# One operation for a softmax step's scaling, a planner that lands loads later, and a second unit's token loads held back, in a planned single-core attention and mixture kernel

## The chip, the cores and the metric

The kernel runs on 1 core of one Trainium2 chip. The metric is the device time of one launch in microseconds (us); lower is better. Before the change three runs gave 815.47, 816.01 and 816.30 us, a median of 816.01 us.

## What is computed

```python
def reference(**kwargs):
    attn_out = _attn_ref(**attn_kwargs)              # 4 x 8 heads x 576 tokens x 64, causal, window 64
    x = attn_out.transpose(0, 2, 1, 3).reshape(2304, 512)
    h = x @ w_in                                     # 2304 x 512 @ 512 x 2048
    P = a[0] + a[1]*h + a[2]*h**2 + a[3]*h**3
    Q = 1.0 + abs(b[0])*abs(h) + abs(b[1])*h**2
    x = (P / (Q + 1e-06)) @ w_out                    # 2048 x 512
    return ((x @ w1) * (x @ w2) @ w3) @ wo2          # 512 x 1024 twice, 1024 x 1024, 1024 x 512
```

## The kernel before, in words

All large products run in split form: each operand is a high part and a low part (a rounded copy and the remainder), and a product is three matmuls (high by high, high by low, low by high).

**Attention and first layer.** Ten units of tokens with four pairs of heads each make 40 attention steps, taken two at a time. A step is: load k, q and v; S, the scores (`sp`, L612); per window of 128x128 a masked copy on DVE with its row minimum (L615) and an exponential on ACT with its row sum (L621); once for two steps a sum on POOL (L554) and a reciprocal on DVE (L557); then the scaling `nm` of each window by that reciprocal, on ACT (L626) or, for the first 16 steps only, on POOL (L628); T, the transpose (`tp`, L633); its copy on ACT (L638); O, the product with v (`op`, L564); and at the end of the two steps the high part x on ACT (L574) and the low part on DVE (L577). A step has 3 windows (tokens in blocks of 384) or 4 (blocks of 512).

The first layer goes over five blocks of tokens (384, 384, 512, 512, 512) and 16 chunks of the hidden dimension for each, two chunks making a pair: 40 pairs. H (`hp`, L689) computes hidden values into PSUM; ACT and DVE evaluate P/Q (L701, L706, L711, L714, L717, L726, L730 to L756). `hi` (L745 or L747) writes the high part of the value to `g[:,0]`, `d` (L754 or L756) computes the remainder's factor `u`, and `lo` (L761) writes the low part `g[:,1] = u * r`. Blocks of 384 have two `lo` of 128x384 for a pair, each on DVE or POOL; in four of the blocks of 512 a flag `whole` makes it one DVE operation of 128x1024. D (`acc`, L767) sums g @ w_out in PSUM, and evictions (L841, L847 and ACT) bring the result to DRAM as `x2d`. In the meantime the weights are split by ACT and DVE (`wt`, L447 to L463), partly stored back to DRAM as `kw` and `kb`.

**Second layer.** w3 @ wo2 is formed first (W: `wp`, L934). Then 768 tokens at a time make a unit u = 0, 1, 2. P(u) forms x @ w1 and x @ w2 in a form with seven products in place of eight (`pa`, `pb`, `pc`, L1079): for each n = 0..7 two stored halves of the weights are loaded ("first" and "second", `wc<-kw`, L1036), and the blocks `bs<-kb` (L1040), from which DVE makes sums `ss` (L1047). The tokens come as four blocks B12, B11, B22 and B21 (`xf`, L1006), split on ACT (L1010) and DVE (L1013), and their sums T1 to T4 (L975) replace them in their buffers. The product of the two results goes through R (L1206) to the output. The order is P0, P1, R0, R1, P2, R2. Sums of the W product are stored and reloaded (`wsum`, L1146).

**What sets the order.** Nothing is reordered at run time. A planner (class `Plan`) holds every operation with its candidate engines, a cost, a `tail` (how long after its end a load's reader may start), an optional due time and the ring of buffers that it fills. It draws noise on the due times from a seeded generator, runs its own list schedule forwards and backwards for some rounds, and keeps the shortest. The result is one fixed order of instructions for each engine. SP issues all DMAs, in that order: a DMA whose buffer or source isn't ready holds every DMA behind it.

```python
rng = Random(60)
due = [d + rng.gauss(0.0, 0.5) for d in dues(preds)]
```

Of the kernel before, what the change touches and what calls it, by code (L numbers as in the profile page):

```python
# [65 lines left out]
class Plan:  # L66
# [30 lines left out]
    def order(self, rounds=16):  # L97
# [125 lines left out]
        rng = Random(60)  # L223
# [21 lines left out]
def body(ctx: ExitStack, tc: tile.TileContext, qkv, kv0, qk0, w_in, w_out, a, b, w1, w2, w3t, wo2, out):  # L245
# [51 lines left out]
    op("c", (("D", 0.95),), constants, tail=2.2, due=8.0)  # L297
# [25 lines left out]
    BEFORE = {NF * PAIRS[t + 1][0] + PAIRS[t + 1][1]: [("O", i + 1) for i in now if i % NP] for t, now in AT.items() if now and t >= 16 and t + 1 < NI}  # L323
# [58 lines left out]

    UN = NT // (2 * T_)
# [44 lines left out]
    def conv(name, dst, n, src, tag, due=None, spare=False, pre=None, kept=None):  # L428
# [62 lines left out]
        op((name, n, "load"), (("D", 1.72),), load, after=["swap"] if spare else [], new=(ws,), tail=2.2, due=due)  # L491
# [40 lines left out]
    def attn(pair):  # L532
# [46 lines left out]
        def step(k):  # L579
# [62 lines left out]
            op(("load", i), (("D", (0.48 if k else 1.12) if thin else 1.1 * wide),), load, after=[("load", i0)] if thin and k else (), new=(kb_,) if thin and k else (kb_, qb), uses=(qb,) if thin and k else (), tail=2.2)  # L642
            op(("loadv", i), (("D", 0.66 * wide),), loadv, after=(("load", i),), new=(vb,), tail=2.2)
# [27 lines left out]
    def chunks(c0):  # L671
# [9 lines left out]
        whole = j >= G  # L681
# [135 lines left out]
    def evacuate(j, part, then):  # L817
# [99 lines left out]
    SPARE = [("w3", 0), ("w3", 2)]  # L917
# [78 lines left out]
    def tokens(u):  # L996
# [24 lines left out]
        for i, (b, (k, h)) in enumerate(where.items()):  # L1021
            j = 2 * u + h
            op(("xl2", u, b), (("D", 1.3),), lambda _, b=b: load(b), after=["swap2"] + [("store", i, int(i in HALVED), n) for n in (2 * k, 2 * k + 1) for i in range(NB) if START[i] < (j + 1) * T_ and START[i] + TOKENS[i] > j * T_], new=(fb[b],), tail=2.2, turn=seq["P", u, 0, 1] - 20.0 + i)
        seven((u,), f, fb, {b: ("xl2", u, b) for b in where}, split)

    def weights(u, n):
# [31 lines left out]
        for i in range(2):  # L1058
            op(("sw", u, n, i), (("D", 1.72),), lambda _, i=i: load(i), after=[(("w1", "w2")[i], n, "keepw"), "swap2"], new=(wbs[i],), tail=2.2)
# [284 lines left out]
```

## Time and profile before

| | us |
|---|---|
| three runs | 815.47, 816.01, 816.30 |
| the profiled execution's own time | 815.19 |
| its span in the trace | 813.4 |
| TensorE (PE) busy | 785.7 (97%) |
| VectorE (DVE) busy | 728.7 (90%) |
| ScalarE (ACT) busy | 553.1 (68%) |
| GpSimd (POOL) busy | 50.1 (6%) |
| mean granted TensorE clock | 0.992 |

The span runs from the first to the last instruction. Busy time is the time in which an engine has an instruction in hand; PE's part is modelled and holds matmuls that overlap. The granted clock is a share of 2.4 GHz: 0.5 is 1.2 GHz, and a window's mean says how much of it was at either level. Idle time is named by what ended it. SP has no busy time of its own; what counts there is when it issues.

### The profile page before, as it was taken

The numbers are of one execution on the slowest core, as the hardware profiler recorded it, in microseconds if no ns is written. First come the engines' busy times: TensorE is split into PE (matmuls) and PEld (weight loads), VectorE is DVE, ScalarE is ACT, GpSimd is POOL, SyncE is SP. The second block draws the span as 40 slices with busy tenths as digits, with TensorE's granted clock in tenths as the row PEclk, the third lists the DMA queues.
The fourth block names the chain that finished last, engine by engine and source line by source line (L and its number), as shares of the span: only waits on it lengthen the run. The fifth ranks groups of instructions, "written<-read, shape, count | busy, mean of one in ns | idle before, by whom it ended". The sixth has DMA issues, their size and how long they took to land.

```text
span 813.4 us, 13444 instructions
## 1 busy us (share of the span) xinstructions
PE 785.7 (97%) x4728; PEld 718.9 (88%) x4728; DVE 728.7 (90%) x1340; ACT 553.1 (68%) x1182; POOL 50.1 (6%) x74
## 2 busy tenths in 40 slices
PE   5879999999999999999999999998999999999998
PEld 4669999888899999888788888888999999999998
DVE  7899999999997999999999998997999798847754
ACT  6888998768999999766477781376565447444434
POOL 2231120001210100000000000000000000000000
PEclk9899999999999999999999999999999999999999
DMA  8977984333167675545763356868979685136402
GB/s 295 337 259 251 306 295 162 119 124 104 64 208 229 222 219 192 180 166 196 288 218 132 143 199 214 306 207 274 316 276 318 234 282 175 64 121 212 156 1 77
DMA packets 64099, 165.51 MB, mean 203 GB/s; under 512 B 7200, under 2 KB 24608, under 8 KB 64032
## 3 DMA queue, kind: packets, MB, share of 16 engines
q1 hardware_dynamic: 64032, 164.66, 59.2%
q8 instruction: 37, 0.61, 0.3%
q14 instruction: 30, 0.25, 0.1%
HBM read 123.21 MB, written 41.42 MB: 202 GB/s over the span
## 4 chain that ended last, share of the span: by engine, by line
PE 86%; DVE 9%; DMA 2%; ACT 2%; issue 1%; POOL 0%; SPq 0%; POOLq 0%; DVEq 0%
PE acc L767 22%; PE hp L689 21%; PE pb L1079 9%; PE pa L1079 6%; PE pc L1079 6%; PE wp L934 5%; PE pb L1206 5%; PE pc L1206 3%; PE pa L1206 3%; PE sp L612 2%; PE tp L633 1%; PE op L564 1%; DMA wc<-kw 1%; DVE wt L453 1%; DMA ws<-in_w_in 1%; DVE u L756 1%
## 5 line engine op out<-in xcount | busy, mean ns | idle before, releaser
L689 PE MATMUL hp<-x,wc 128*128 128x512 f32 (+1 forms) x960 | 220.1, 374 | 3.0 <-DVE u L717 3.0
L767 PE MATMUL acc<-g,wc 128*128 128x512 f32 (+1 forms) x960 | 215.0, 371 | 4.4 <-POOL g L761 3.6
L767 PEld LDWEIGHTS acc<-g,wc 128*128 128x128 f32 x960 | 174.3, 188 | 28.9 <-POOL g L761 4.0
L689 PEld LDWEIGHTS hp<-x,wc 128*128 128x128 f32 x960 | 174.9, 190 | 26.6 <-DVE u L717 3.9
L1079 PE MATMUL pb<-xb,wc 128*128 128x384 f32 x432 | 86.0, 336 | 0.3 <-ACT u L1087 0.3
L1079 PEld LDWEIGHTS pb<-xb,wc 128*128 128x128 f32 x432 | 76.5, 189 | 0.7 <-ACT u L1087 0.6
L621 ACT ACTIVATE sm<-sm,st 128x128 f32<-128x128 f32 x144 | 56.4, 400 | 18.3 <-DVE st L615 18.2
L730 ACT ACTIVATE r<-qa,cq 128x1024 f32<-128x1024 f32 (+1 forms) x40 | 42.9, 1072 | 30.7 <-DVE qa L726 16.9
L711 ACT ACTIVATE u<-hp,ca 128x512 f32<-128x512 f32 (+1 forms) x80 | 59.5, 745 | 3.0 <-PE hp L689 3.0
L1079 PE MATMUL pa<-xb,wc 128*128 128x384 f32 x288 | 58.1, 339 | 2.5 <-DMA wc<-kw 2.5
L706 ACT ACTIVATE qa<-hp,cb 128x512 f32<-128x512 f32 (+1 forms) x80 | 51.7, 646 | 12.7 <-PE hp L689 12.1
L1079 PE MATMUL pc<-xb,wc 128*128 128x384 f32 x288 | 57.3, 334 | 0.0
L1168 ACT ACTIVATE rt<-prod 128x768 fp32r<-128x768 f32 x42 | 35.6, 847 | 31.5 <-PE pa L1206 10.3
L1171 DVE TENSOR_TENSOR rt<-prod,rt 128x768 fp32r<-128x768 f32 x42 | 40.1, 956 | 16.6 <-ACT rt L1168 16.1
L701 ACT ACTIVATE h<-hp 128x512 f32<-128x512 f32 (+1 forms) x80 | 44.5, 556 | 14.0 <-PE hp L689 11.1
L1079 PEld LDWEIGHTS pa<-xb,wc 128*128 128x128 f32 x288 | 51.3, 191 | 3.0 <-ACT ww L943 2.8
L460 ACT ACTIVATE wc<-wt 128x512 fp32r<-128x512 f32 x48 | 30.1, 633 | 32.9 <-DVE wt L453 23.5
L726 DVE SCALAR_TENSOR_TENSOR qa<-h,cab,qa 128x1024 f32<-128x1024 f32 (+1 forms) x40 | 47.4, 1185 | 4.6 <-ACT qa L706 3.7
L1079 PEld LDWEIGHTS pc<-xb,wc 128*128 128x128 f32 x288 | 50.5, 188 | 0.0
L450 DVE SCALAR_TENSOR_TENSOR wt<-ws,wt 128x512 uint32<-128x512 uint32 x72 | 50.0, 697 | 0.4
L453 DVE SCALAR_TENSOR_TENSOR wt<-ws,wt 128x512 uint32<-128x512 uint32 x72 | 49.2, 686 | 0.3
L612 PE MATMUL sp<-k,q 64*64 64x128 f32 (+1 forms) x384 | 40.7, 297 | 8.5 <-DMA k<-in_kv 6.3
(86 smaller groups left out, 1370.6 us busy)
## 6 DMA issues: line engine op xcount, KB each, us to landing
wc<-kw SPq DMA_DIRECT2D x48, 512.0 KB, 5.3
bs<-kb SPq DMA_DIRECT2D x24, 512.0 KB, 4.4
ws<-in_w_in SPq DMA_DIRECT2D x16, 512.0 KB, 5.4
ws<-in_w_out SPq DMA_DIRECT2D x16, 512.0 KB, 4.8
ws<-in_w SPq DMA_DIRECT2D x16, 512.0 KB, 4.5
kw<-ws SPq DMA_DIRECT2D x16, 512.0 KB, 3.2
ws<-in_w3t SPq DMA_DIRECT2D x16, 512.0 KB, 4.5
wsum<-wsum SPq DMA_DIRECT2D x16, 512.0 KB, 5.7
```

The source lines that it names most:

```text
L450: stt(out=x["b"], in0=x["st"][:, :, 0], scalar=29, in1=x["b"], op0=ALU.logical_shift_right, op1=ALU.bitwise_or)
L453: stt(out=x["b"], in0=x["st"][:, :, 1], scalar=0xC0000000, in1=x["b"], op0=ALU.bitwise_and, op1=ALU.bitwise_or)
L612: nc.tensor.matmul(sp[h, w, :], x["q"][h, w], x["k"][h, kat[w] * W_:kat[w] * W_ + P], start=True, stop=True)
L621: act(x["sm"][:, m, :], x["sm"][:, m, :], AF.Exp, bias=col(0, k, m), scale=-1.0, accum_out=col(1, k, m))
L689: nc.tensor.matmul(x["hp", m], wf_(win, f0 + m)[:, s_, kk * P:(kk + 1) * P], (xh, xl)[m_][xk][:, kk, :], start=(kk == 0 and i == 0), stop= ...
L701: act(x["h2"][:, m, :], x["hp", m], AF.Square)
L706: act(x["qa"][:, m, :], x["hp", m], AF.Abs, scale=b0)
L711: act(x["u"][:, m, :], x["hp", m], AF.Identity, scale=a3, bias=a2)
L726: stt(out=x["qa"], in0=x["h2"], scalar=b1, in1=x["qa"], op0=MUL, op1=ADD)
L767: nc.tensor.matmul(accs[j, part, n], wf_(wout, f0 + m)[:, s_, n * P:(n + 1) * P], x["g"][:, m_, m, :], start=(first and i == 0), stop=(las ...
L1079: nc.tensor.matmul(x[m], sws[u, n, i0][:, s_, (c0 + k) * P:(c0 + k + 1) * P], t[:, m_, k, :], start=(first and k == 0 and i == 0), stop=(k ...
L1206: nc.tensor.matmul(x[m, n], w[:, s_, (c + n) * P:(c + n + 1) * P], rts[u, b, r][:, m_, k, :], start=(first and r == 0 and k == 0 and i == ...
```

## The change

The scaling of a step becomes one operation in the plan, on one engine: ACT (still one instruction for each window), or one `tensor_tensor` over all windows on POOL or DVE, with the reciprocals broadcast. `whole` becomes False, so the low part of a pair of 512 tokens is two operations, each on DVE or POOL. The planner gets `tail=3.0` for loads in place of 2.2, another seed, other places of the attention steps among the pairs (`AT`), no O steps placed ahead of the following H (`BEFORE`), earlier due times for evictions, other due times for the `wsum` sums and w2, and another spare buffer. The loads of the second unit's tokens (u = 1) may not be issued before the second half-load of n = 3 of the first unit (`XL = 3`). What is computed stays the same; every engine's order changes. Nearly all of the code moves down by one line, L628 and after by two for a few lines (the scaling on POOL is L630).

```diff
-        rng = Random(60)
+        rng = Random(65)
...
-        AT[((-8, -6, -4, -2), (0, 1, 2, 3), (4, 5, 6, 7), (15, 16, 17, 18), (20, 22, 24, 26))[j][r // 2]].append(i)
+        AT[((-8, -6, -4, -2), (0, 1, 2, 3), (4, 5, 6, 6), (16, 18, 19, 20), (22, 24, 25, 26))[j][r // 2]].append(i)
...
-    BEFORE = {... for t, now in AT.items() if now and t >= 16 and t + 1 < NI}
+    BEFORE = {... for t, now in AT.items() if now and t >= 99 and t + 1 < NI}
...
-            def nm(m, e):
-                r, t = col(3, k, m), x["sm"][:, m, :]
+            def nm(e):
+                r = y["st"][:, 2 * NW * 3 + NW * k:2 * NW * 3 + NW * k + NW]
                 if e == "A":
-                    act(t, t, cp, scale=r)
+                    for m in range(NW):
+                        act(x["sm"][:, m, :], x["sm"][:, m, :], cp, scale=r[:, m:m + 1])
                 else:
-                    nc.gpsimd.tensor_scalar(out=t, in0=t, scalar1=r, scalar2=1.0, op0=MUL, op1=MUL)
+                    engine[e].tensor_tensor(out=x["sm"], in0=x["sm"], in1=r.unsqueeze(2).to_broadcast([P, NW, P]), op=MUL)
...
-            for m in range(NW):
-                op(("nm", i, m), (("A", 0.32), ("P", 0.52)) if i < 16 else (("A", 0.32),), lambda e, m=m: nm(m, e), after=(("rc", i0),), uses=(sb, mb))
+            op(("nm", i), (("A", 0.32 * NW), ("P", 0.97 * wide), ("V", cost(0.065, 0.40))), nm, port=True, after=(("rc", i0),), uses=(sb, mb))
...
-        whole = j >= G
+        whole = False
...
-            due = seq[then[:-1] + (n,)] - 0.7
+            due = seq[then[:-1] + (n,)] - 1.4
...
-    SPARE = [("w3", 0), ("w3", 2)]
+    SPARE = [("w3", 0), ("w3", 5)]
...
-            op(("xl2", u, b), (("D", 1.3),), ..., after=["swap2"] + [("store", ...) ...], new=(fb[b],), tail=2.2, turn=...)
+            op(("xl2", u, b), (("D", 1.3),), ..., after=["swap2"] + ([("sw", 0, XL, 1)] if u == 1 else []) + [("store", ...) ...], new=(fb[b],), tail=3.0, turn=...)
...
-            op(("sw", u, n, i), (("D", 1.72),), lambda _, i=i: load(i), after=[...], new=(wbs[i],), tail=2.2)
+            op(("sw", u, n, i), (("D", 1.72),), lambda _, i=i: load(i), after=[...], new=(wbs[i],), tail=3.0)
...
-        due = seq["P", 0, 1, 1] + 8.0 * i
+        due = seq["P", 0, 1, 1] + 6.0 * i
...
-        conv("w2", w2c, n, w2[n], None, pre=231.0 + 32.0 * n, kept=1)
+        conv("w2", w2c, n, w2[n], None, pre=231.0 + 35.0 * n, kept=1)
```

All other loads get `tail=3.0` in the same way.

In the whole program the change turns 123 scaling windows on ACT into 80, and 21 on POOL into none; 12 whole-step scalings appear on DVE (5 of 128x384, 7 of 128x512) and 6 on POOL (3 and 3). Of the low parts, DVE has 35 of 128x512 in place of 16 of 128x1024 and 11 of 128x512, and 10 of 128x384 in place of 16; POOL has 22 of 128x384 in place of 16 and 13 of 128x512 in place of 5. PE's matmuls are the same in number and shape.

Three places show how the order moves. On SP, at the start of P(0), where the loads of the second layer's weights are issued (`kw2` is the stored weights of n = 2, `bs` its blocks, `xf` tokens), before:

```order
L1036 DMA wc_5605<-kw0_2804 128x1024
...
L1006 DMA xf_5681<-x2d_58 128x2x384
...
L1040 DMA bs_5703<-kb1_2869 128x1024
L1036 DMA wc_5722<-kw1_2892 128x1024
L1036 DMA wc_5741<-kw0_2804 128x1024
L1040 DMA bs_5808<-kb2_3226 128x1024
L1036 DMA wc_5831<-kw2_3311 128x1024
L1036 DMA wc_5847<-kw1_2892 128x1024
L1006 DMA xf_5872<-x2d_58 128x2x384
L1146 DMA wsum00_5888<-wsum_5822 128x1024
L1036 DMA wc_5912<-kw3_3747 128x1024
```

and now:

```order
L1041 DMA bs_5642<-kb1_2750 128x1024
L1037 DMA wc_5658<-kw1_2774 128x1024
L1037 DMA wc_5671<-kw0_2668 128x1024
L1007 DMA xf_5686<-x2d_58 128x2x384
L1037 DMA wc_5754<-kw2_3102 128x1024
L1041 DMA bs_5770<-kb2_3002 128x1024
L1037 DMA wc_5792<-kw1_2774 128x1024
L1147 DMA wsum00_5817<-wsum_5780 128x1024
L1147 DMA wsum01_5836<-wsum_5783 128x1024
L1037 DMA wc_5859<-kw3_3660 128x1024
```

The first load of `kw2` stood behind the blocks `bs` of n = 2 and stands ahead of them now; `xf_5872` of the second unit is gone from here (its first row comes 13 rows behind the last one shown), and the last block of the first unit, `xf_5686`, has moved behind the second load of `kw0`.

On PE, the rows ahead of the first two `acc` of the program, before:

```order
L612 MATMUL sp<-k,q 64x128 x12
L689 MATMUL hp<-x,wc 128x384 x15
L633 MATMUL tp<-idn,sm 128x128 x3
L689 MATMUL hp<-x,wc 128x384 x3
L633 MATMUL tp<-idn,sm 128x128 x3
L689 MATMUL hp<-x,wc 128x384 x6
L564 MATMUL op<-sm,v 64x64 x24
L689 MATMUL hp<-x,wc 128x384 x6
L612 MATMUL sp<-k,q 64x128 x12
L767 MATMUL acc_805<-g,wc 128x384 x3
L767 MATMUL acc_812<-g,wc 128x384 x3
```

and now:

```order
L613 MATMUL sp<-k,q 64x128 x12
L690 MATMUL hp<-x,wc 128x384 x18
L635 MATMUL tp<-idn,sm 128x128 x6
L565 MATMUL op<-sm,v 64x64 x24
L690 MATMUL hp<-x,wc 128x384 x15
L613 MATMUL sp<-k,q 64x128 x12
L690 MATMUL hp<-x,wc 128x384 x21
L768 MATMUL acc_839<-g,wc 128x384 x3
L768 MATMUL acc_849<-g,wc 128x384 x3
```

From the program's start to its first `acc` PE had 48 `hp` matmuls and has 72 now, with the same 84 scores, 36 transposes and 72 products with v.

On DVE, the rows from a pair's `d` on whose low part POOL computes (`g_2173` before, both halves of the pair of `u_3806` now), before:

```order
L750 SCALAR_TENSOR_TENSOR qa_2093<-qa_2093,g_2173 128x1024
L447 TENSOR_SCALAR wt_2196<-ws_1731 128x512
L756 SCALAR_TENSOR_TENSOR u_2048<-u_2048,ca_63,qa_2093 128x1024
L447 TENSOR_SCALAR wt_2209<-ws_2055 128x512
L761 TENSOR_TENSOR g_2173<-u_2048,r_2151 128x512
L714 TENSOR_TENSOR u_2204<-u_2204,hp_2132 128x512
```

and now:

```order
L757 SCALAR_TENSOR_TENSOR u_3806<-u_3806,ca_63,qa_3819 128x1024
L616 ISA sm_3959,st_3942<-sp_3958,mask_77 128x128
L616 ISA st_3942 128x1
...
L718 SCALAR_TENSOR_TENSOR u_3932<-u_3932,ca_63,hp_3880 128x512
L715 TENSOR_TENSOR u_3932<-u_3932,hp_3919 128x512
```

DVE had a conversion and its own half of the low part behind `d`, both on SBUF operands; it has masked copies out of PSUM there now (four of them, two of which are left out with their second rows), and both halves are on POOL.

## Rows read from the trace of the kernel before

**Rows 1.** The page, part 1: busy time, share and instructions of each engine.
```profile
PE 785.7 (97%) x4728; PEld 718.9 (88%) x4728; DVE 728.7 (90%) x1340; ACT 553.1 (68%) x1182; POOL 50.1 (6%) x74
```
**Rows 2.** Windows: each engine's busy time, PE's granted clock, DMA share and GB/s.
```profile
0.00:60.00 60.00, 41.00 (x410) 34.31 (x411) 51.26 (x166) 47.90 (x156) 17.00 (x40) 0.91 0.84 295
60.00:90.00 30.00, 30.00 (x245) 28.97 (x244) 27.53 (x75) 26.17 (x77) 4.60 (x8) 1.00 0.81 280
90.00:110.00 20.00, 18.43 (x162) 16.97 (x161) 19.90 (x51) 18.58 (x57) 3.47 (x4) 1.00 0.84 287
110.00:340.00 230.00, 230.00 (x1464) 209.03 (x1464) 221.99 (x432) 198.97 (x470) 24.99 (x23) 1.00 0.52 172
340.00:350.00 10.00, 9.22 (x97) 7.29 (x96) 10.00 (x14) 6.48 (x11) 0.00 (x0) 1.00 0.59 204
350.00:550.00 200.00, 199.94 (x891) 166.18 (x890) 195.30 (x256) 122.74 (x185) 0.00 (x0) 1.00 0.58 206
550.00:560.00 10.00, 7.48 (x35) 7.19 (x34) 7.06 (x16) 6.32 (x14) 0.00 (x0) 0.83 0.99 311
600.00:610.00 10.00, 9.73 (x56) 9.41 (x56) 9.92 (x19) 6.96 (x14) 0.00 (x0) 1.00 0.81 279
```
**Rows 3.** Timeline of PE, 540 to 562 us; idle time ahead in brackets.
```profile
550.11 2.25 PE L1079 MATMUL pb<-xb,wc 128*128 128x384 f32 x12
554.88 2.26 PE L1079 MATMUL pa<-xb,wc 128*128 128x384 f32 x6 [2.52 <-DMA wc<-kw]
```
**Rows 4.** Timeline of SP's queue, 500 to 560 us: start and length of issues.
```profile
534.31 0.85 SPq L1036 DMA_DIRECT2D wc<-kw  x2
545.20 0.32 SPq L1040 DMA_DIRECT2D bs<-kb  x1
545.61 1.68 SPq L1036 DMA_DIRECT2D wc<-kw  x2
547.40 0.37 SPq L1006 DMA_DIRECT2D xf<-x2d  x1
```
**Rows 5.** Waits of SP's queue, 533 to 556 us: total, times, longest.
```profile
SPq L1040 <- DVE ss L1047: 6.0, 1, 6.0
SPq L1040 <- DMA bs<-kb: 3.9, 1, 3.9
```
**Rows 6.** The chain that ended last, 535 to 562 us: start, length, what.
```profile
545.61 9.13 DMA wc<-kw
```
**Rows 7.** Groups by line and form: busy us, mean ns of one.
```profile
L626 ACT ACTIVATE sm<-sm,st 128x128 f32<-128x128 f32 x123 | 39.3, 401 | 0.2
L628 POOL TENSOR_SCALAR sm<-sm,st 128x128 f32<-128x128 f32 x21 | 10.3, 504 | 4.9 <-DVE st L557 4.9
L761 DVE TENSOR_TENSOR g<-u,r 128x1024 fp32r<-128x1024 f32 x16 | 19.5, 1220 | 0.0
L761 DVE TENSOR_TENSOR g<-u,r 128x384 fp32r<-128x384 f32 x16 | 9.5, 613 | 0.0
L761 DVE TENSOR_TENSOR g<-u,r 128x512 fp32r<-128x512 f32 x11 | 7.8, 732 | 0.0
L761 POOL TENSOR_TENSOR g<-u,r 128x384 fp32r<-128x384 f32 x16 | 17.3, 1088 | 84.6 <-DVE u L756 50.5 <-DVE u L754 32.8 <-DVE st L557 1.1
L761 POOL TENSOR_TENSOR g<-u,r 128x512 fp32r<-128x512 f32 x5 | 7.5, 1516 | 69.5 <-DVE u L756 28.4 <-ACT u L711 20.7 <-DVE u L754 20.4
L447 DVE TENSOR_SCALAR wt<-ws 128x512 uint32<-128x512 uint32 x72 | 31.6, 442 | 0.8 <-DMA ws<-in_w_in 0.6 <-DMA ws<-in_w 0.2
```
**Rows 8.** Timeline, 195 to 200 us: start, length, engine, line.
```profile
195.88 3.06 POOL L761 TENSOR_TENSOR g<-u,r 128x512 fp32r<-128x512 f32 x2 [20.44 <-DVE u L754]
...
197.71 1.52 DVE L447 TENSOR_SCALAR wt<-ws 128x512 uint32<-128x512 uint32 x1
```
**Rows 9.** Timeline of PE at two gaps before 110 us.
```profile
55.94 1.90 PE L767 MATMUL acc<-g,wc 128*128 128x384 f32 x6 [2.94 <-POOL g L761]
...
92.57 2.35 PE L689 MATMUL hp<-x,wc 128*128 128x384 f32 x12 [0.42 <-DVE u L717]
```

More of the change, by code (lines that the diff above doesn't have):

```diff
@@ L321, in body @@
     TS, TT, TO, TOO = 0.67, 0.33, (0.71, 0.42), 1.9
-    BEFORE = {NF * PAIRS[t + 1][0] + PAIRS[t + 1][1]: [("O", i + 1) for i in now if i % NP] for t, now in AT.items() if now and t >= 16 and t + 1 < NI}
+    BEFORE = {NF * PAIRS[t + 1][0] + PAIRS[t + 1][1]: [("O", i + 1) for i in now if i % NP] for t, now in AT.items() if now and t >= 99 and t + 1 < NI}
     seq = {}
@@ L489, in keepw @@
             nc.sync.dma_start(out=kw[n][:, kept], in_=x["w"].bitcast(F32))
-        op((name, n, "load"), (("D", 1.72),), load, after=["swap"] if spare else [], new=(ws,), tail=2.2, due=due)
+        op((name, n, "load"), (("D", 1.72),), load, after=["swap"] if spare else [], new=(ws,), tail=3.0, due=due)
         op((name, n, "b0"), (("V", 0.34),), b0_, port=True, after=((name, n, "load"),), new=(wt,), uses=(ws,), turn=None if due is None else due + 4.0)
@@ L499, in conv @@
                 op((name, n, "keepd"), (("D", 1.72),), keepd, after=((name, n, "lo"),), uses=(wc,), tail=2.0, due=seq["H", NF + n, 0])
-                op((name, n, "second"), (("D", 1.72),), second, after=((name, n, "keepd"),), new=((tag, (name + "2", n)),), tail=2.2)
+                op((name, n, "second"), (("D", 1.72),), second, after=((name, n, "keepd"),), new=((tag, (name + "2", n)),), tail=3.0)
         else:
@@ L861, in evacuate @@
                 after.append(("evl", j, n))
-                op(("evl", j, n), (("D", 0.66 * ev_cost),), lambda _, n=n: load(n), after=(("store", j, 0, n), "swap"), new=(vb,), tail=2.2)
+                op(("evl", j, n), (("D", 0.66 * ev_cost),), lambda _, n=n: load(n), after=(("store", j, 0, n), "swap"), new=(vb,), tail=3.0)
             elif more:
@@ L865, in evacuate @@
                 if n % 2 == 0:
-                    op(("evl", j, n // 2), (("D", 1.3 * ev_cost),), lambda _, n=n: load(n), after=(("store", j, 0, n), ("store", j, 0, n + 1)), new=(vb,), tail=2.2)
+                    op(("evl", j, n // 2), (("D", 1.3 * ev_cost),), lambda _, n=n: load(n), after=(("store", j, 0, n), ("store", j, 0, n + 1)), new=(vb,), tail=3.0)
             new = new and not more
@@ L1022, in tokens @@
             j = 2 * u + h
-            op(("xl2", u, b), (("D", 1.3),), lambda _, b=b: load(b), after=["swap2"] + [("store", i, int(i in HALVED), n) for n in (2 * k, 2 * k + 1) for i in range(NB) if START[i] < (j + 1) * T_ and START[i] + TOKENS[i] > j * T_], new=(fb[b],), tail=2.2, turn=seq["P", u, 0, 1] - 20.0 + i)
+            op(("xl2", u, b), (("D", 1.3),), lambda _, b=b: load(b), after=["swap2"] + ([("sw", 0, XL, 1)] if u == 1 else []) + [("store", i, int(i in HALVED), n) for n in (2 * k, 2 * k + 1) for i in range(NB) if START[i] < (j + 1) * T_ and START[i] + TOKENS[i] > j * T_], new=(fb[b],), tail=3.0, turn=seq["P", u, 0, 1] - 20.0 + i)
         seven((u,), f, fb, {b: ("xl2", u, b) for b in where}, split)
@@ L1160, in wc_sums @@
             op(("wsk", i, q), (("D", 1.72),), lambda _, q=q: keep(q), after=(("wsp", i, q),), uses=(wbs[q],), tail=2.0, due=due + 6.0)
-            op(("wsl", i, q), (("D", 1.72),), lambda _, q=q: again(q), after=(("wsk", i, q),), new=(("wa", ("wsum", i, q)),), tail=2.2, turn=seq["R", 0, 1, 0, 0] + 4 * q + i)
+            op(("wsl", i, q), (("D", 1.72),), lambda _, q=q: again(q), after=(("wsk", i, q),), new=(("wa", ("wsum", i, q)),), tail=3.0, turn=seq["R", 0, 1, 0, 0] + 4 * q + i)
     rts = {}
```

15 lines of the change are left out of this document (8 added, 7 removed).

## The prediction

> **What bounds the kernel now.** I read the busy shares first, then the windows, then PE's timeline at the places where the windows show PE idle, and last the queue that the idle time points to. PE is busy for 785.7 of 813.4 us [rows 1], and the windows say where the rest lies [rows 2]: 19.0 us of idle time in the first 60 us, 1.57 in 90 to 110, 0.78 in 340 to 350, 2.52 in 550 to 560, 0.27 in 600 to 610; from 110 to 340 there is none, from 350 to 550 only 0.06. The reader should see two things. Work taken off any other engine gains nothing where PE is full, so this change can gain only at those five places. And PE's clock costs besides: a mean of 0.91 over the first 60 us and of 0.83 from 550 to 560 [rows 2], 2.4 GHz in part and 1.2 GHz in part; in the second window (1 - 0.83) x 10 = 1.7 us of full-speed work is lost. DVE is second: 222.0 of 230 us in 110 to 340 and 195.3 of 200 in 350 to 550 [rows 2]. It makes the values that PE's `acc` needs and has little room to be late.
>
> The profiled execution took 815.19 us, 0.8 under the median of 816.01. I add the terms to 815.19 and then these 0.8.
>
> **The place that decides: 552 to 560 us.** PE ends a row of `pb` at 552.36, waits 2.52 us for `wc<-kw`, and resumes at half clock: six matmuls take 2.26 us there [rows 3], where twelve take 2.25 ahead of the wait. The load is the first one of n = 2. It was issued only at 545.61 and took 9.13 us to land [rows 4, 6]. The issue was late because SP had been silent since 535.2 [rows 4]: it stood before the `bs` load of n = 2, for 3.9 us because of a DMA and for 6.0 us because of DVE's sums `ss` [rows 5]. The load of `kw2` behind it needs neither. The change puts that load ahead of the `bs` in SP's order, and takes the second unit's `xf`, which went out at 547.40 into the same traffic [rows 4], out of this stretch. With nothing blocked ahead of it, it can be issued about when SP came free before, at 535 to 536. If it lands as slowly as it did, in 9.13 us, it is there at 545, and its matmuls are due at about 551 to 552. So the wait goes, and the clock with it: 2.52 + 1.7 = **4.2 us**. The bounds: nothing, if another load is late in its place; 4.2 at most, as there is no more idle time in this window. What is late next: the second load of n = 1 is still queued behind the blocked `bs`, and the first unit's last block B21, whose load now comes after the second load of `kw0`, is needed after some 6 us more of DVE's work than before. I give back 0.5 us for these (0 to 4.2).
>
> **The scaling and the low parts.** ACT loses 43 windows of 0.401 us, 17.2 us [rows 7]. ACT is not what PE waits for after 110 us, so this is worth nothing there. DVE: 16 whole low parts go (19.5 us), 24 halves come (24 x 0.732 = 17.6), 6 of 128x384 go (6 x 0.613 = 3.7), and 12 scalings come, which no row shows; a multiplication of that size out of SBUF is the low part itself, so 5 x 0.613 + 7 x 0.732 = 8.2 [rows 7]. That makes DVE 2.6 us longer; the scalings read one operand broadcast, so I bound each between half and twice that price (-1.5 to +10.8). POOL gains 9 x 1.088 + 11 x 1.516 = 26.5 us and loses 10.3 [rows 7]; its share stays small, but a low part on POOL ends 0.4 to 0.8 us later than on DVE, in the path from `d` to `acc`. I priced every instruction of both orders by its own row's duration and compared DVE's work up to a pair's `d` with PE's work up to that pair's first `acc`. The largest lag is the same (17.6 us before, in the first pair, 17.7 now, in the seventh); it grows by 1 to 5 us in the pairs 5 to 22 (11.6 to 16.4 in pair 7) and shrinks by 4 to 6 in the pairs 23 to 26. The latter removes the 0.78 us at 340 to 350 (**-0.8**; 0 to 0.8). The former runs through the stretch in which PE has no idle time but the 1.57 us of 90 to 110, two waits of which are 0.42 for DVE [rows 9] and 0.64 for POOL: I take **+0.7** (-1.6, if that idle time goes, to +4).
>
> By the rows POOL also holds DVE up. While two low parts of 128x512 ran on POOL from 195.88 to 198.94, a conversion on DVE took 1.52 us [rows 8], in place of the 0.442 of its kind [rows 7]. At the places where POOL takes a low part, a DVE operation on SBUF operands alone stands among the first two behind `d` in 6 of 16 cases before and in 6 of 22 now; in the others there are operations that read PSUM. At 1.1 us each that is the same on both sides, so I add nothing; the other end, POOL's longer work of 26.5 - 10.3 = 16.2 us passed on to DVE in full, is a rival below. The Trainium skill (SBUF — State Buffer, SBUF: two separate sides) says that DVE and GpSimd share a pair of ports under an exclusive lock, so that a DVE operation with two SBUF inputs, or in a 2-port mode, stands still for the whole of a GpSimd operation. The trace agrees at 197.71; by this rule, wherever such an operation is next, all that POOL gains is DVE's loss.
>
> **The start.** In the first 60 us DVE and ACT run almost without a pause (51.3 and 47.9 us busy [rows 2]), and PE waits for them. Priced the same way, DVE's work up to the third pair of tokens' `x` grows from 23.2 to 25.2 us, which starts the first `hp` that needs it 2.0 us later, and up to the first `d` from 45.4 to 47.9. Against this PE has 24 more `hp` ahead of the first `acc`. Twelve take 2.2 us [rows 9], so these are 4.4 us of work, in a place where PE waited 2.94 us and then ran at half clock (six `acc` in 1.90 us [rows 9]). The first `acc` was at 55.94; with these 4.4 us of work done it would have been at 60.3, or at 62.0 with the same 1.7 us of clock as at 552. For the change I find the first `acc` at 60.9: the sixth chunk's `hp`, behind DVE's fourth operation on `u`, starts at about 58.7 by the same pricing, and 2.2 us of work follow. With part of the low clock remaining I take **-0.5** (-3 to +2.5). The earlier evictions, the spacing of `wsum` and of w2, and the other spare buffer move operations on engines and queues with room while PE is full: nothing, as long as no buffer comes free late.
>
> **P(0) to P(1).** The second unit's tokens are issued some 15 to 30 positions later on SP. Three of the four blocks stay about ten us ahead of their need; the last is as tight as it was, and PE waited 0.27 us there [rows 2]: 0 (0 to 4).
>
> **Sum:** -4.2 + 0.5 - 0.8 + 0.7 - 0.5 = -4.3 us on 815.19, so 810.9, and **811.7** as a median.
>
> **Rivals.**
> - **DVE comes too late from 60 to 340 us (chance 0.16; slower).** The scalings on DVE, the longer low parts on POOL and the lags that are up by 1 to 5 us open waits ahead of `acc`. For: DVE is busy 96% of this stretch, and waits of that kind exist at 90 to 110. Against: the largest lag is unchanged, and PSUM reads stand beside POOL now. It decides where a `d` comes over some 2 us later against PE than before. If five or six pairs wait 1.2 us each, that is +7 us in place of +0.7, so 818.0.
> - **POOL holds DVE up in full (0.04; slower).** As at 197.71 [rows 8], but for the whole 16.2 us, of which about half shows on PE, since the other half falls to `d`s that are early: 811.7 + 8 = 819.7. For: DVE's full windows leave no empty place. Against: the order puts PSUM reads beside POOL. It is what the Trainium skill's rule (SBUF — State Buffer, SBUF: two separate sides) would give without that order.
> - **The wait at 552 us is only moved (0.13; same).** The second load of n = 1 or the split of B21 comes as late as `kw2` did. For: both still hang on the same DVE sums. Against: more PE work lies ahead of them. Nothing is gained there: 811.7 + 3.7 = 815.4.
> - **The held tokens are late at the second unit (0.07; same).** A load of 9.13 us [rows 6] that misses its place by 2.5 us costs what it did at 552, a wait and the clock, 4.2 us: 815.9.
> - **The start gains more (part of the forecast).** If the 2.94 us wait and its clock go, 809.
>
> **Numbers.** Forecast 0.60, all of it faster. About 0.2% (1.6 us) is what a measurement of this kernel can tell from no change. The rivals give 0.20 slower and 0.20 about the same, of which I move 0.02 to faster and 0.01 to slower, because part of a gap may stay. The range reaches from 808.0 (start and 90 to 110 us gain in full) to 818.0 (the first rival); the forecast's own range is 808.5 to 814.
>
> **What would show it.** Right: no idle time and clock 1.00 in the windows between 540 and 570 us; SP issues the first `kw2` load before the blocked `bs`; PE's idle time to 60 us at 18 to 20; none at 340 to 350; ACT's scaling near 26 us in place of 39.3. Wrong: new waits of PE for `g` or `u` between 60 and 340 us that sum to over 3 us; a wait for `xb` or `wc` and a clock under 1.00 somewhere between 540 and 620; or more idle time or a lower clock in the first 60 us than 19.0 and 0.91.

## The result, and the profile after

The changed kernel took 807.72 us (median of 4 runs, 806.66 to 808.58) against 816.15 before (4 runs): a ratio of 0.9894, 95% interval 0.9877 to 0.9911, a gain of 8.4 us. The forecast was 811.7 us, its range 808.0 to 818.0: the direction was right, the forecast gain of 4.3 us about half of what came, and the time lies just below the range. On two of the chips of the experiments the changed kernel gave 808.35 against 814.95 (e5: 0.9911, interval 0.9893 to 0.9928) and 807.20 against 815.04 (e15: 0.9904, 0.9884 to 0.9923), 6.6 and 7.8 us.

The windows of the changed kernel, with the columns of [rows 2]; the profiled execution took 807.59 us, its span was 805.8:

```profile
0.00:60.00 60.00, 40.72 (x412) 32.90 (x413) 52.05 (x167) 46.71 (x151) 7.85 (x23) 0.94 0.84 290
60.00:90.00 30.00, 30.00 (x244) 29.15 (x243) 29.74 (x74) 26.44 (x73) 6.58 (x9) 1.00 0.85 296
90.00:110.00 20.00, 20.00 (x179) 19.65 (x178) 20.00 (x61) 19.33 (x59) 2.11 (x4) 1.00 0.89 305
110.00:340.00 230.00, 229.12 (x1450) 207.28 (x1449) 223.01 (x432) 189.38 (x430) 33.29 (x33) 1.00 0.50 169
340.00:350.00 10.00, 10.00 (x104) 8.39 (x103) 9.12 (x13) 9.92 (x22) 0.00 (x0) 1.00 0.35 125
350.00:540.00 190.00, 189.88 (x839) 156.69 (x838) 186.76 (x256) 114.55 (x170) 7.66 (x6) 1.00 0.63 221
540.00:570.00 30.00, 30.00 (x173) 29.78 (x172) 29.35 (x60) 20.95 (x42) 0.00 (x0) 1.00 0.85 291
600.00:620.00 20.00, 20.00 (x117) 20.00 (x116) 18.88 (x38) 10.38 (x20) 0.00 (x0) 1.00 0.87 302
```

PE has no wait and its full clock from 540 to 570; the waits of 90 to 110, 340 to 350 and 600 to 610 are gone too. New are 0.88 us between 110 and 340 and 0.12 from 350 to 540. The first 60 us hold 19.3 us of idle time in place of 19.0. SP issues the first load of `kw2` at 530.08, ahead of the `bs` (SP's queue of the changed kernel):

```profile
530.08 0.42 SPq L1037 DMA_DIRECT2D wc<-kw  x1
538.75 0.32 SPq L1041 DMA_DIRECT2D bs<-kb  x1
```

The groups that the change touches (line, engine, operation, shape; busy us, mean ns), against [rows 7]:

```profile
L628 ACT ACTIVATE sm<-sm,st 128x128 f32<-128x128 f32 x80 | 25.5, 397 | 0.6 <-DVE st L558 0.5
L630 DVE TENSOR_TENSOR sm<-sm,st 128x512 f32<-128x512 f32 x7 | 4.8, 684 | 0.0
L630 DVE TENSOR_TENSOR sm<-sm,st 128x384 f32<-128x384 f32 x5 | 2.8, 551 | 0.0
L630 POOL TENSOR_TENSOR sm<-sm,st 128x512 f32<-128x512 f32 x3 | 3.7, 1220 | 0.8 <-DVE st L558 0.8
L630 POOL TENSOR_TENSOR sm<-sm,st 128x384 f32<-128x384 f32 x3 | 2.5, 832 | 2.1 <-DVE st L558 2.1
L762 DVE TENSOR_TENSOR g<-u,r 128x512 fp32r<-128x512 f32 x35 | 24.0, 719 | 0.1
L762 POOL TENSOR_TENSOR g<-u,r 128x384 fp32r<-128x384 f32 x22 | 22.2, 1031 | 155.5 <-PE tp L635 62.3 <-DVE u L757 35.4 <-DVE u L755 34.7
L762 POOL TENSOR_TENSOR g<-u,r 128x512 fp32r<-128x512 f32 x13 | 18.8, 1460 | 84.8 <-DVE u L757 54.4 <-ACT sm L622 11.0 <-ACT u L712 9.7
L448 DVE TENSOR_SCALAR wt<-ws 128x512 uint32<-128x512 uint32 x72 | 30.7, 432 | 0.5 <-DMA ws<-in_w_in 0.5
```

The whole-step scalings cost 0.551 and 0.684 us on DVE, where I had put 0.613 and 0.732. POOL's are cheaper than its low parts of the same size. ACT's scaling fell by 13.8 us of busy time, not by the 17.2 forecast: neighbouring windows overlap in the record, so that 123 of them were busy for 39.3 us [rows 7], 0.32 each.

**A finer account.** Busy time hides small slowness, and the first 60 us differ between executions of one program. (e5 and e15 are the changed kernel again and e6 the kernel before, with one blank line more in the file.) So I took the start of each of the 4,728 matmuls in a trace and subtracted its kind's usual distance to the next (0.173 us for 384 columns, 0.227 for 512; the three small kinds 0.031, 0.071 and 0.117; in all some 770 us of work, the same for both kernels). What is left is PE's loss, waits and low clock together. Cut by the work done so far, in us:

| trace | start (0 to 55) | 55 to 120 | 120 to 300 | 300 to 350 | 350 to 500 | 500 to 560 | 560 to end | behind the start |
|---|---|---|---|---|---|---|---|---|
| before | 29.1 | 3.0 | 0.5 | 1.3 | 0.4 | 4.5 | 1.0 | 10.6 |
| before, again (e6) | 29.9 | 3.0 | 0.5 | 1.3 | 0.5 | 3.7 | 1.5 | 10.4 |
| after | 28.6 | 0.1 | 2.2 | 0.6 | -0.1 | 0.2 | 0.4 | 3.5 |
| after, again (e5) | 31.0 | 0.1 | 2.2 | 0.6 | -0.1 | 0.2 | 0.4 | 3.4 |
| after, third (e15) | 28.3 | 0.1 | 2.2 | 0.6 | -0.1 | 0.2 | 0.4 | 3.4 |

Behind the start the two kernels repeat to within 0.2 us, but for the place at 500 to 560 and the end of the old one, and differ by 7.1 us. The start differs by 2.7 us between three executions of one program. Work of 55 to 120 is the time of some 80 to 150 us, 500 to 560 that of some 535 to 600. All further comparisons use this account besides the times.

### The profile page after: what moved, and what is told of

The parts are those of the page before. It is cut to its first block, busy times and chain, and to the rows that moved or that the text cites. A ratio compares the mean times of both kernels' runs of the same rounds, so it can differ in the third digit from the quotient of the medians.

```text
span 805.8 us, 13408 instructions
## 1 busy us (share of the span) xinstructions
PE 782.1 (97%) x4728; PEld 715.9 (89%) x4728; DVE 726.9 (90%) x1352; ACT 543.9 (68%) x1141; POOL 57.5 (7%) x73
## 4 chain that ended last, share of the span: by engine, by line
PE 70%; DVE 22%; ACT 5%; issue 2%; POOL 1%; DMA 1%; SPq 0%; ACTq 0%; DVEq 0%; POOLq 0%
PE acc L768 15%; PE hp L690 15%; PE pb L1080 9%; PE pa L1080 6%; PE pc L1080 6%; PE wp L935 5%; PE pb L1207 5%; PE pc L1207 3%; PE pa L1207 3%; DVE sm L616 2%; DVE wt L451 2%; DVE u L718 2%; DVE u L757 2%; DVE u L715 2%; DVE g L748 2%
## 5 line engine op out<-in xcount | busy, mean ns | idle before, releaser
L690 PE MATMUL hp<-x,wc 128*128 128x512 f32 (+1 forms) x960 | 217.7, 373 | 5.0 <-ACT qa L707 2.2
L768 PE MATMUL acc<-g,wc 128*128 128x512 f32 (+1 forms) x960 | 212.8, 369 | 0.1
L762 POOL TENSOR_TENSOR g<-u,r 128x384 fp32r<-128x384 f32 (+1 forms) x35 | 41.0, 1190 | 240.3 <-DVE u L757 89.8
```

What stands on the lines that cost most here:

```text
L690: nc.tensor.matmul(x["hp", m], wf_(win, f0 + m)[:, s_, kk * P:(kk + 1) * P], (xh, xl)[m_][xk][:, kk, :], start=(kk == 0 and i == 0), stop= ...
L762: engine[e].tensor_tensor(out=x["g"][:, 1, m], in0=x["u"][:, m], in1=x["r"][:, m], op=MUL)
L768: nc.tensor.matmul(accs[j, part, n], wf_(wout, f0 + m)[:, s_, n * P:(n + 1) * P], x["g"][:, m_, m, :], start=(first and i == 0), stop=(las ...
```

## The experiments

The kernel before was measured beside every experiment on the same chip; that is the time each one is held against, and times of different chips are compared only loosely. Some kernels move operations in the planner's finished list and leave the rest of the order; others are planned anew ("replanned").

**The place at 552 us.** e1 moves one load of the kernel before:

```diff
+        todo = plan.order()
+        at = {o["key"]: o for o in todo}
+        todo.remove(at["sw", 0, 2, 0])
+        todo.insert(todo.index(at["bs", 0, 2]), at["sw", 0, 2, 0])
```

> The kernel before with its own order, but the first load of n = 2 one place earlier on SP, ahead of the blocks bs of n = 2. If the blocked queue alone made the wait at 552 us, the load is issued at about 535.5 instead of 545.6, PE's 2.52 us wait and the half clock behind it go, and the time falls by 4.2 us, to 812.0. If the wait only moves to the next load or to the split tokens, another wait of over 1 us stands between 550 and 575 us and the time falls by less than 1.5 us.

It took 812.91 us against 814.45 (0.9985, interval 0.9973 to 0.9996), a gain of 1.5 us where 4.2 were expected. The wait at 552 us is gone, but PE's timeline shows another one ahead of it:

```profile
537.15 6.19 PE L934 MATMUL wp<-wc 128*128 128x512 f32 x26 [0.83 <-DVE wc L463]
```

A second profile of the kernel before (one run, 815.81 us) says that the move did not make this wait.

> The kernel before once more, for a second profile. If the wait at 552 us is the same in every execution, 2.5 us of idle time and 1.7 us of half clock stand there again. If it comes and goes with the landing of one load, both are clearly smaller or larger, which would explain why moving the load gave 1.2 us and not 3.0. The first 70 us may differ by 2 us or more.

Its PE timeline (lines one further down):

```profile
536.80 6.19 PE L935 MATMUL wp<-wc 128*128 128x512 f32 x26 [0.93 <-DVE wc L464]
556.50 1.28 PE L1080 MATMUL pa<-xb,wc 128*128 128x384 f32 x6 [2.01 <-ACT ww L944]
```

Here the kernel before waits 0.93 us for DVE and 2.01 us at the place of [rows 3], and six matmuls take 1.28 us: no half clock. The place costs 4.5 us in one execution and 3.7 in another. e1 has 1.3 us there, most of it at 537, so the load's place in the queue carried 2.4 to 3.2 us of it.

e2 does the reverse to the changed kernel:

```diff
+        todo.remove(at["sw", 0, 2, 0])
+        todo.insert(todo.index(at["bs", 0, 2]) + 1, at["sw", 0, 2, 0])
```

> The changed kernel with the first load of n = 2 put back behind the blocks bs of n = 2. There the bs is issued at 538.75 and the first matmul that needs the load starts at 547.39. If the place in the queue is the whole cause, the wait comes back, 2 to 4 us slower than the changed kernel (810 to 812). If DVE's earlier sums, which free the bs at 538.75 instead of 545.20, are a second and sufficient cause, the load is issued at 539.2, lands in its usual 5 us and the time stays within 0.8 us of 807.7.

It took 808.53 us against 814.45 (0.9927, 0.9911 to 0.9942), the time of the changed kernel, with 0.2 us at 500 to 560. SP's queue and PE in e2:

```profile
539.26 0.32 SPq L1041 DMA_DIRECT2D bs<-kb  x1
539.67 0.86 SPq L1037 DMA_DIRECT2D wc<-kw  x2
```
```profile
547.72 1.20 PE L1080 MATMUL pa<-xb,wc 128*128 128x384 f32 x6
```

The load is issued at 539.67 behind the `bs`, is needed at 547.72, and nobody waits. In the new plan DVE frees the buffer of the `bs` at 539 and not at 545 (the `bs` in [rows 4]). So there are two cures for the wait at 552, the load's place in the queue and, in the new plan, the earlier sums.

The late issue was not enough for this wait by itself. e10 below still issues the load behind the `bs`, and 1.8 us later than the kernel before:

```profile
547.43 0.86 SPq L1036 DMA_DIRECT2D wc<-kw  x2
```

There the first of these two loads lands in 4.7 us, and PE has no wait between 540 and 620. In the kernel before it took 9.1 us, and 8.5 in its second profile (e6). Why it landed so slowly there is open.

**Draw or rules.** e3 and e4 exchange the seeds, e16 tries a third one (`Random(65)` and `Random(60)`, and 61).

> The kernel before with nothing changed but the planner's seed, 65 for 60. Its order on SP has the first load of n = 2 ahead of the bs. If the gain is mostly the draw of the plan, 808 to 812.5, with no wait at 552. If it is the rules (one scaling operation, the halves, later landing, the hold), no better than 814.5.

> The changed kernel with the old seed, 60. If the rules carry the gain, 806.5 to 809.5. If the draw carries it, 811 or more, with new waits of PE somewhere between 60 and 620 us.

> The changed kernel with seed 61. If the rules carry the gain, 806.5 to 810.5, with no wait between 540 and 570 us; if seed 65 was a lucky draw, 812 or more.

| kernel | seed | us | before | ratio (interval) | start | 55 to 120 | 500 to 560 | behind the start |
|---|---|---|---|---|---|---|---|---|
| e3, rules of before | 65 | 814.74 | 814.45 | 0.9993 (0.9977 to 1.0009) | 30.8 | 3.2 | 1.6 | 8.7 |
| e4, rules of after | 60 | 809.57 | 814.45 | 0.9940 (0.9918 to 0.9962) | 29.7 | 1.6 | 0.3 | 4.7 |
| e16, rules of after | 61 | 807.23 | 815.04 | 0.9915 (0.9888 to 0.9942) | 27.0 | 1.4 | 0.1 | 3.8 |

Behind the start the new rules lose 3.4 to 4.7 us with three seeds, the old ones 10.6 and 8.7 with two. The draw moves some 1 to 2 us there; the rules carry the gain. The place at 552 is another matter: e3, with the old rules, has no wait there either (of its 1.6 us at 500 to 560 some 1.0 lie at 537, with a wait of 0.74 us for DVE), and it takes as long as the kernel before. That wait belonged to one plan.

**The scaling and the halves, in the fixed new order.** e5 is the changed kernel on this chip (808.35 us).

> The changed kernel once more, on the chip of these runs, so that the others can be held against it. By the profile, PE's waits and half clock behind the first 70 us are 1.0 us in place of 6.9, so 5.9 us below the kernel before; what goes beyond that would have to come from the first 70 us.

e7 gives all scalings back to ACT, e8 the 13 halves of 512 tokens on POOL to DVE; the order stays.

```diff
+        for o in todo:
+            if o["key"][0] == "nm":
+                o["engine"] = "A"
```

> The changed kernel with its own order, but the 18 scalings that it has on DVE and POOL done by ACT again, window by window: 64 more ACT instructions of 0.40 us, 25.6 us. If the merged scaling carries the gain, 2 to 6 us slower than the changed kernel, with new waits of PE before 130 us. If the order and the queue carry it and ACT has room, within 1 us.

e7 took 816.95 us against 814.95 (1.0021, 1.0012 to 1.0031), and 8.6 more than the changed kernel. That is more than the 2 to 6 us expected. Its loss is 3.4 at 55 to 120 and 5.3 at 120 to 300, in place of 0.1 and 2.2. ACT's scaling is busy for 44.6 us in place of 25.5. PE's timeline and the chain that ended last, 140 to 160 us (start, length, what):

```profile
157.42 2.05 PE L613 MATMUL sp<-k,q 128*128 128x128 f32 x16 [1.71 <-ACT sm L640]
```
```profile
144.99 0.57 ACT h L702
145.57 2.33 ACT sm L628 x8
147.90 0.58 ACT qa L707
148.51 1.30 DVE qa L727
149.89 1.17 ACT r L731
```

Eight scaling windows (2.33 us) stand in the middle of the chain, between the hidden values `h` and `qa` that ACT prepares for DVE. The chain goes on over ACT up to the copy (L640) that ends PE's wait at 157.42: with the windows, ACT is what PE waits for here.

```diff
+        for o in todo:
+            if o["key"][0] == "lo" and o["key"][1] >= 2 * NF and o["engine"] == "P":
+                o["engine"] = "V"
```

> The changed kernel with its own order, but the 13 low parts of 128x512 that it has on POOL done by DVE: 13 x 0.69 = 9 us more work on DVE, spread over 140 to 480 us. If DVE's work bounds that stretch, PE waits 4 to 9 us more there. If the values are early enough, as the lags said of most pairs, under 2 us more; each low part is then even 0.8 us earlier than on POOL.

e8 took 813.04 us (0.9980, 0.9967 to 0.9992), 4.7 more than the changed kernel; its loss is 3.0 us larger at 300 to 350 and 1.1 at 350 to 500. PE waits there that the changed kernel doesn't have:

```profile
343.44 0.96 PE L690 MATMUL hp<-x,wc 128*128 128x512 f32 x3 [1.21 <-ACT qa L707]
382.61 5.73 PE L690 MATMUL hp<-x,wc 128*128 128x512 f32 x24 [0.79 <-DVE u L718]
```

About half of the 9 us that DVE got reached PE.

**One rule added, one rule left out; all replanned.** e9 is the kernel before with the scaling alone, e10 with the halves alone; e11, e12, e17 and e18 are the changed kernel without the scaling, the halves, the hold of the second unit's loads, and the later landing.

```diff
-        whole = j >= G
+        whole = False
```

(e10; e12 is the reverse.) e17 and e18:

```diff
-... after=["swap2"] + ([("sw", 0, XL, 1)] if u == 1 else []) + [("store", ...
+... after=["swap2"] + [("store", ...
```
```diff
-tail=3.0
+tail=2.2
```

> The kernel before with one rule of the change, the scaling as one operation on ScalarE, GpSimd or VectorE, planned anew with the old seed. If the scaling by itself lets the planner find an order without waits, PE's waits at 90 to 110 and at 552 us are gone and it comes to 808 to 811. If it needs the other rules, no better than 813.

> The kernel before with one other rule, the low parts of 512 tokens as two operations on DVE or POOL, planned anew with the old seed. If relief of DVE is what counts, 809 to 812, with the wait at 346 us gone. Its SP order still has the first load of n = 2 behind the bs, so a wait near 552 us would say that the halves don't touch that place.

> The changed kernel without the new scaling (window by window on ACT, or POOL in the first 16 steps), all other parts kept, planned anew with the new seed. If the scaling carries the gain behind the start, its waits between 60 and 320 us grow by over 2 us, to 811 or more; if a new plan makes up for it, within 1.5 us of 808.4.

> The changed kernel with the low parts of 512 tokens as one DVE operation again, all other parts kept, planned anew with the new seed. In the fixed order, giving the halves back to DVE cost 4.7 us. If that price is one of DVE's work, 811 to 814 here; if it was only the price of an order made for the halves, within 1.5 us of 808.4.

> The changed kernel without the hold on the second unit's token loads, planned anew. They go out on SP among the loads of n = 2 and 3 again. If the hold is what closes the place, PE loses 1.5 to 4 us between 530 and 575 us, or at the second unit, and it comes to 809.5 to 812; if not, within 1.5 us of 807.8.

> The changed kernel with the planner's landing of loads at 2.2 again, planned anew. The rows give 4.5 to 5.7 us from issue to landing, so a plan made for 2.2 should find loads late: if that is what closes the place, waits for a DMA of 1.5 us or more between 500 and 610 us and 809.5 to 813; if the other rules do it, within 1.5 us of 807.8.

| kernel | us | before | ratio (interval) | start | 55 to 120 | 120 to 300 | 300 to 350 | 500 to 560 | 560 to end | behind the start |
|---|---|---|---|---|---|---|---|---|---|---|
| e9, only scaling | 811.98 | 815.25 | 0.9948 (0.9930 to 0.9967) | 28.5 | 1.5 | 2.2 | 0.2 | 2.0 | 1.9 | 8.3 |
| e10, only halves | 812.24 | 815.25 | 0.9944 (0.9920 to 0.9969) | 29.1 | 2.9 | 2.5 | 0.3 | 1.6 | 0.7 | 8.1 |
| e11, no scaling | 819.78 | 815.25 | 1.0044 (1.0027 to 1.0061) | 35.0 | 3.0 | 2.6 | 2.4 | 0.2 | 1.9 | 10.1 |
| e12, no halves | 812.83 | 815.25 | 0.9966 (0.9945 to 0.9988) | 33.5 | 1.6 | 0.7 | 0.3 | 0.2 | 0.9 | 3.9 |
| e17, no hold | 813.49 | 814.37 | 0.9990 (0.9981 to 1.0000) | 32.1 | 0.2 | 0.9 | 2.3 | 1.3 | 2.6 | 7.3 |
| e18, old landing | 809.08 | 814.37 | 0.9932 (0.9915 to 0.9948) | 29.9 | 1.3 | 0.9 | 1.0 | 0.2 | 0.4 | 3.5 |

e9 and e10, one rule each, gain about 3 us: neither rule carries the gain alone. e9 lies between its two expected ranges. Its 2.0 us at 500 to 560 are mostly a wait of 1.35 us for another load, at 569 us; e10's 1.6 hold a wait of 0.70 us for DVE at 536.

The column of 55 to 120 sorts the plans by one rule. All with the whole-step scaling lose 0.1 to 1.6 us there (the changed kernel, e4, e9, e12, e16, e17, e18), all without it 2.9 to 3.2 (the kernel before, e3, e10, e11). The column of 120 to 300 shows no such order.

Without the scaling the new rules are worse than the kernel before. Two waits of e11's PE timeline, one in the start, one in the middle:

```profile
48.19 1.33 PE L690 MATMUL hp<-x,wc 128*128 128x384 f32 x3 [3.11 <-DVE u L718]
349.22 2.05 PE L613 MATMUL sp<-k,q 128*128 128x128 f32 x16 [0.89 <-ACT sm L639]
```

The second wait ends on ACT; of e11's eight waits between 60 and 400 us five end on DVE. Without the halves the plan is nearly as good behind the start (3.9), and what it loses lies in the start, among it one wait:

```profile
59.93 1.94 PE L690 MATMUL hp<-x,wc 128*128 128x384 f32 x6 [2.99 <-DVE u L718]
```

The halves are in blocks of 512 tokens alone, and the hold is in the second layer, so neither stands in the start; that e12 and e17 lose 33.5 and 32.1 us there is a matter of the new plan. One plan without a rule is thus a rough price of the rule.

Without the hold, the second unit's tokens are issued among the weights again, and the second pass through the weights finds a load late:

```profile
544.52 3.92 SPq L1007 DMA_DIRECT2D xf<-x2d  x2
```
```profile
603.85 1.31 PE L1080 MATMUL pc<-xb,wc 128*128 128x384 f32 x6 [0.23 <-DVE u L1091]
619.08 1.14 PE L1080 MATMUL pa<-xb,wc 128*128 128x384 f32 x5 [1.16 <-DMA wc<-kw]
```

From 500 on it costs 3.9 us (1.3 + 2.6) in place of 0.6. The whole takes 813.49 us, more than the 809.5 to 812 expected. But PE does not wait at 552 here either; most of the 1.3 us lies between 571 and 579. And the load that is late at 619 was issued at 612.75, when PE had just freed its buffer, and landed in 6.3 us; the second unit's four token loads had all landed by 604.7. So the plan is worse without the hold, but that the tokens stood in the weights' way is not shown. The later landing is worth nothing measurable behind the start. The places of the attention steps (`AT`), `BEFORE`, the due times and the spare buffer were not tried one by one.

**The start.** e13 puts transposes of the identity into three of PE's waits there, e14 into seven, so that PE idles less; e15 is the changed kernel beside them.

```diff
+            if o["key"][0] == "H" and o["key"][2] == 0:
+                heads += 1
+                n = {3: 18, 5: 6, 6: 11}.get(heads, 0)
+                if n:
+                    spare = psum.tile([P, P], F32, tag="at", bufs=2, name="fill")
+                    for _ in range(n):
+                        nc.tensor.transpose(spare, idn, idn)
```

> The changed kernel with 18, 6 and 11 transposes of the identity put into PE's three waits ahead of hp at 42.2, 52.9 and 57.9 us (2.21, 0.83 and 1.35 us long), into a PSUM tile that nobody reads. If the low clock behind 44 us follows from the wait and costs time, the granted clock stays at 1.00 from 40 us on and the time falls by 1 to 2 us. If PE waits for DVE and ScalarE there anyway, the clock may stay up but the time does not move by over 0.8 us.

> As e13, with 43 more idle matmuls in the four longest waits before 26 us. If PE's clock rises by what PE does, it is at its full level earlier than the 11 to 16 us (counted from the start) of the changed kernel and has no low stretch up to 60 us; the time falls by 2 to 4 us if the start is bound by PE's speed, by less than 1 us if by DVE and ScalarE, which are busy for 98 of 100 there. If the added work delays the scores, slower.

> The changed kernel again, on the chip of these runs: 807.5 to 809.

e13 took 808.56 us (0.9921, 0.9904 to 0.9938), e14 810.13 (0.9937, 0.9919 to 0.9955), e15 807.20, against 815.04. Windows of e13:

```profile
20.00:30.00 10.00, 7.18 (x84) 5.57 (x84) 9.96 (x37) 8.92 (x34) 1.24 (x3) 0.77 0.90 325
30.00:40.00 10.00, 9.70 (x77) 7.66 (x74) 9.19 (x28) 8.16 (x28) 1.52 (x2) 0.72 0.74 252
40.00:50.00 10.00, 9.51 (x103) 8.54 (x103) 9.87 (x29) 9.18 (x28) 0.20 (x1) 1.00 0.89 323
```

The clock is full from 40 to 50 us, where it was 0.83 in the changed kernel (0.84 in e5), but it is so in e15 too (1.00), without any filling, and it is low from 20 to 40 instead. Over the first 60 us it is 0.91 in e13 and e14 and 0.94, 0.89 and 0.94 in the three profiles of the changed kernel. So the filling did not raise the clock, and it gained nothing. DVE is busy for 9.96 of 10 us from 20 to 30, which speaks for a start that waits for DVE and ACT. What a full clock would be worth there is not shown. The three runs of e5 and e15 with a mean clock of 1.000 took 806.03 to 807.23 us, the four with 0.991 to 0.994 took 808.05 to 809.95, and the five between (0.996) 805.79 to 809.30; from the first two groups some 2 us is an estimate. No version beat the changed kernel by more than the scatter of its own runs (e16's 807.23 is the same).

## Why the prediction was wrong in size

Step by step, forecast against the account of losses:

- **The place at 552 us: 4.2 less 0.5 forecast; 3.5 to 4.3 measured (4.5 and 3.7 before, 0.2 after).** Its size held. The half clock was there in one profile of the kernel before and not in the other, where more waiting stood in its place. The cause was only half right: I had put it all on the load's place in SP's queue. e1 shows that this carries 2.4 to 3.2 us; e2 shows that the new plan doesn't need it; e10 shows that a load issued as late is in time when it lands in 4.7 us and not in 9.1. No other plan waits at 552, with the old rules or the new, so the wait belonged to one plan. What the new rules add is that nothing else is lost nearby: with all of them, or with all but the scaling, the halves or the late landing, 0.1 to 0.3 us at 500 to 560, without the hold (e17) 1.3, with the old rules, or one new rule among them, 1.6 to 4.5.
- **60 to 340 us: +0.7 forecast, about -1.2 measured (3.0 to 0.1 at 55 to 120, 0.5 to 2.2 at 120 to 300). This is the step that failed,** 1.9 of the 4.0 us by which the forecast was too high. I had compared DVE's work with PE's and put the relief of ACT at nothing, with "ACT is not what PE waits for after 110 us". None of PE's waits between 60 and 340 us ended on ACT in the trace before ([rows 9] has two of them), but a chain may run through ACT and end on DVE, and I did not follow one. e7 refutes that: with the windows back on ACT in the same order, PE loses 6.5 us more behind the start, and the chain runs through ACT's scaling windows. Where the planner is free, the gain at 55 to 120 comes with the whole-step scaling: a loss of 0.1 to 1.6 us with it, of 2.9 to 3.2 without it, whatever the other rules are. e11 says the same of the whole: without the scaling, the other rules lose 10.1 us behind the start in place of 3.4, and take 819.78 us, 4.5 more than the kernel before. The chain through ACT itself is shown for the order of e7 alone. The forecast loss is there too, in another place: 120 to 300 costs 1.7 us more than before, in part waits of 0.38 us for ACT at 149.71 and 0.42 for DVE at 175.03; it is not tied to one rule. The halves on POOL are worth 4.8 us in the new order (e8) and 0.5 behind the start when the planner is free to answer (e12, 3.9 against 3.4).
- **340 to 350 us: -0.8 forecast, -0.7 measured** (300 to 350: 1.3 to 0.6).
- **P(0) to P(1) and the rest: 0 forecast, about -1.1 measured**: 0.4 to -0.1 at 350 to 500, and 1.0 (1.5 in the second profile) to 0.4 at the end. I had feared that the held tokens come late; PE has no wait between 540 and 620, so they did not. Of e17's 2.6 us at the end, without the hold, the cause is open.
- **The start: -0.5 forecast; not resolved.** Three executions of the changed kernel lost 28.3 to 31.0 us, two of the kernel before 29.1 and 29.9. The first `acc` came at 61.4 us (63.9 and 61.1 in e5 and e15), where the forecast had 60.9. The sign of failure that I had named, more than 19.0 us of idle time or a clock under 0.91, can't tell: the changed kernel has 19.3 and 0.94 in one profile, 17.0 and 0.89 in another.
- **The offset: 0.8 added.** The profiled execution of the kernel before was one of its faster ones, that of the changed kernel (807.59) lies at its median, so these 0.8 us did not carry over.

Behind the start the account falls by 7.1 us. The rest of the 8.4 on the first chip lies within what the start and the chips move.

Of the rivals, "DVE comes too late" did not happen: the only wait for DVE between 60 and 340 us is the 0.42 at 175.03, and DVE's busy time fell from 728.7 to 726.9 us. "POOL holds DVE up in full" did not either. POOL's low parts and scalings took 12.1 us more than its low parts and windows before, where I had put 16.2; its busy time grew by 7.4 only, as one sum (L554) that had taken 5.5 us takes under 0.8 now. Its low parts got shorter (1.031 and 1.460 us in place of 1.088 and 1.516), and so did DVE's conversions (0.432 in place of 0.442). By the Trainium skill (SBUF — State Buffer, SBUF: two separate sides) only a DVE operation with two SBUF inputs or in a 2-port mode stands still beside a GpSimd one. The durations agree with that: DVE operations on SBUF operands alone ran beside POOL's low parts for 10.8 of their 25.0 us before and for 9.6 of 41.7 now, the others beside them read PSUM.

## What to carry to other kernels

Put the relief of an engine at nothing only after you have followed the chains through it: ACT was 68% busy, none of PE's waits between 60 and 340 us ended on it, and still 19 us of short windows put back on it cost 6.5 us in an order made without them, because they stood between two steps of one chain. Where a planner writes the whole order, undo an edit in the fixed order and also replan without it: the first gives what the order now leans on, the second what the rule is worth, give or take what a new plan moves elsewhere. Look up where a loss lies before you give it to a rule: a sum over 60 us of work put four different waits into one column here. And compare executions by PE's loss place by place; here it repeated to 0.2 us where whole times scattered by 3.

## What the runs showed of the hardware

How long PE's clock stays low at first differs between executions of one program. Twelve score matmuls took 1.54 us in the changed kernel at 18.47, where the granted clock of 18 to 20 us is 0.55 (1.2 GHz for most of it), and 0.87 at full clock (1.00). The changed kernel had 0.87 at 11.85 us, the same program in e5 (its lines are one further down) still 1.54 at 14.27. PE's timeline of the one and of the other:

```profile
11.85 0.87 PE L613 MATMUL sp<-k,q 64*64 64x128 f32 x12 [1.20 <-DMA k<-in_kv]
18.47 1.54 PE L613 MATMUL sp<-k,q 64*64 64x128 f32 x12
```
```profile
14.27 1.54 PE L614 MATMUL sp<-k,q 64*64 64x128 f32 x12 [0.23 <-DVE st L559]
19.42 0.87 PE L614 MATMUL sp<-k,q 64*64 64x128 f32 x12
```

In e5 the windows give a clock of 1.00 from 10 to 20 us, where these twelve still took 1.54, so there the durations tell and the clock's column does not. Six executions of e5 took 806.2 to 810.0 us, with mean granted clocks from 1.000 (806.58) down to 0.991 (809.95). And POOL's multiplication by a broadcast operand took 1.220 us for 128x512 where its plain one took 1.460; on DVE the broadcast one took 0.684, no more than its low part of that size (0.719).
